# Eight result buffers instead of six, softmax weights made in place in PSUM, PSUM banks from a table, and another order of the matmul steps, in a gated mix of local attention and a Mish MLP

## The chip, the cores and the metric

The kernel runs on one core of a Trainium2 chip. The core has a matmul engine (TensorE, PE in the profile; its weight loads are PEld), a vector engine (VectorE, DVE), a scalar engine (ScalarE, ACT), GpSimd (POOL) and a queue engine (SyncE, SP) from which nearly all DMAs are issued. Each engine takes its instructions strictly in the order in which they were written for it, and waits on semaphores where one needs another's result. The matmuls accumulate in PSUM, which is used here as eight banks of 512 floats per partition; all else on the chip lies in SBUF. The metric is the device time of one execution in microseconds; 622.23 is the median of three runs of the kernel before (620.2 to 622.58).

## The reference: a gate between attention and an MLP

```python
S, D, H, Dh, W, dil, F = 2048, 640, 32, 20, 8, 2, 1728      # all fp32
g = sigmoid((x * gate_w).sum(-1, keepdims=True))
# a: each token attends to itself and the 7 tokens 2, 4, ... 14 before it
q, k, v = split_heads(x @ wqkv)
logits = einsum("bhsd,bhswd->bhsw", q, gathered(k)) * Dh ** -0.5      # masked where the index is negative
a = einsum("bhsw,bhswd->bhsd", softmax(logits), gathered(v)) @ wo
# b: dense, Mish, dense
h = x @ w1 + b1
b = (h * tanh(softplus(h))) @ w2
out = g * a + (1 - g) * b
```

Three groups of matrix products carry the work: the projections to q, k and v, the two of the MLP, and the one behind the attention. The attention itself is elementwise products and sums over a window of eight.

## The kernel before

**Matmuls.** An fp32 operand is kept as a pair of reduced-precision parts, a high half and a low half. ACT copies the operand to the high half (L444), and DVE or GpSimd subtracts that from it to get the low half (L447); this is `split`. A product of two pairs is three matmuls, high by high, high by low, low by high (`mm3`, L512 to L514): the stationary operand is the weights' for the MLP, so its low half is first read by the third. Where blocks allow it, the kernel forms a two-by-two block product with seven block products instead of eight. The sums of blocks that this needs are made ahead by DVE or GpSimd (`combined`, L1017), and between the products a partial sum is carried from one PSUM bank into the next: ACT copies a bank to another ("seed", L1144, and L879 in the steps c1), and DVE adds or subtracts a kept block (L826 in `sum_to`, L1162 in `added`).

**Stages.** The 2048 tokens are two halves P of two blocks of 512. The steps have names in a long string, ORDER, which is the order of PE. `u.U.i` is slot i of a unit U of the q, k and v projection (a unit is a quarter of the heads in one half); `p.2.j.a1` to `c3` make units 2 and 3 together by the seven products; `q.P.i.*` are the first MLP layer for a pair i of column groups; `x`, `rest`, `last` and others belong to the second layer and the output. In p.2.j the step a1 makes a block v and a3 a block u, which are stored to HBM (`store`); c0 fetches both again into one pair buffer by two DMAs (L871); c1 seeds a bank with u (ACT L879), accumulates onto it, and DVE makes a second bank as that bank minus v (L826); c2 and c3 go on in the first and second of the two banks. c2 writes the bank that L826 reads, so it can't start before L826 is done.

**Attention on DVE.** For two groups of 128 tokens and eight heads: product with the keys (L569), sum (L572); for four groups: maximum and difference (L590, L591); ACT makes the exponential (L592) and from it the weights times the gate, into a tile `pw` of SBUF (L596); DVE sums, inverts, and multiplies `pw` by the inverse into `pg` in PSUM (L603 to L605); then product with the values (L614, two), sum (L618) and a transpose (L525). ACT copies the queries of two groups to `qg` in PSUM ahead of L569 (L575).

**What sets the order.** PE's order is the string's. For DVE, ACT, GpSimd and SP a planner inside the kernel (`Plan.run`) plays the whole program through with an estimated duration for each task and emits, for each engine, the ready task of the lowest rank; a split or a sum with engine "ANY" goes to DVE or to GpSimd, by when PE will need it. Buffers come in rings, taken in turn and given back when their last reader is done: three banks `sb` and three `qb` of PSUM, 24 pair buffers (NPAIR), eight raw ones (NRAW), six result buffers `hb` (NH) and others. So any change of a ring, an estimate or the string moves instructions on all engines.

**Start.** `warm()` (L424 to L428) issues six matmuls of 512 columns on constants, four of 128 and three of 384, into the three sb banks, while the first DMAs are under way. Unit 0 follows with L708 and L674 (`first_slots`, `qkv_pass`).

## Time and profile before

| | us |
|---|---|
| median of three runs | 622.23 (620.2, 622.23, 622.58) |
| the profiled execution | 620.13 |
| its span | 618.4 |
| PE busy | 611.8 (99%) |
| DVE busy | 584.4 (95%) |
| ACT busy | 364.6 (59%) |
| GpSimd (POOL) busy | 312.0 (50%) |

A row of the timeline has the start and the duration in us, the engine, the line, the operation, the tiles (written, then read) and their shape; `x3` is a row of three instructions in a run, whose duration is from the first start to the last end. In brackets stands the idle time ahead of it and what ended it. Matmuls overlap in the pipeline: a row of one lasts 0.39, and the next starts 0.22 or 0.23 later. In a table by stretches, the numbers behind the two bounds are the busy time and count of PE, PEld, DVE, ACT and POOL, the granted clock, the share of the DMA engines and GB/s. In the waits, a row has the total, the number and the longest.

### The profile page before, as it was taken

Reading aid. Unit: us, or ns where it says so; the run is one execution under the profiler, and the core shown is the slowest. Engines: PE = TensorE matmul, PEld = TensorE weight load, DVE = VectorE, ACT = ScalarE, POOL = GpSimd, SP = SyncE. Lnnn points to the kernel's source line nnn. Section 1 sums busy time; section 2 is a strip of 40 time slices with the busy share of each in tenths; the row PEclk is TensorE's granted clock in tenths of the full one; section 3 lists DMA queues with packets and bytes.
Section 4 is the critical chain, followed back from the end, with each engine's and each line's share of the span. In section 5 each row is a group of like instructions: output and inputs, shape, how many; then the busy total and the mean of one; then the engine's idle time right before and its main releaser. Section 6 shows DMA issues by size and latency. Waiting matters only on the chain.

```text
span 618.4 us, 9150 instructions
## 1 busy us (share of the span) xinstructions
PE 611.8 (99%) x2719; PEld 508.5 (82%) x2719; DVE 584.4 (95%) x550; ACT 364.6 (59%) x854; POOL 312.0 (50%) x287
## 2 busy tenths in 40 slices
PE   9999999999989999999999999999999999999997
PEld 7888888888878888888888888888888888888886
DVE  8899999999999999999999999999999999989955
ACT  7677657666785466533483656867855633645420
POOL 1677748679675446653545327898227634001000
PEclk9999999999999999999999999999999999999999
DMA  9873775979997689996889748978978966889923
GB/s 321 235 217 116 227 253 158 264 237 322 309 288 219 195 253 274 280 265 161 212 249 345 222 122 275 283 197 256 287 245 247 242 175 187 261 270 291 275 86 119
DMA packets 100769, 145.95 MB, mean 236 GB/s; under 512 B 11552, under 2 KB 54560, under 8 KB 100496
## 3 DMA queue, kind: packets, MB, share of 16 engines
q1 hardware_dynamic: 97360, 139.61, 70.9%
q0 software_dynamic: 3072, 5.51, 6.3%
q8 instruction: 21, 0.34, 0.2%
q14 instruction: 28, 0.23, 0.1%
q10 hardware_dynamic: 288, 0.26, 0.1%
HBM read 91.33 MB, written 53.03 MB: 233 GB/s over the span
## 4 chain that ended last, share of the span: by engine, by line
PE 97%; DVE 1%; DMA 0%; issue 0%; SPq 0%; ACT 0%; DVEq 0%; ACTq 0%
PE qb L512 20%; PE qb L514 20%; PE qb L513 20%; PE sb L512 12%; PE sb L514 12%; PE sb L513 12%; PE qb L674 1%; PE sb L426 1%; DMA o<-ot 0%; DVE lg L572 0%; PE sb L519 0%; PE sb L518 0%; PE qb L519 0%; PE qb L518 0%; PE sb L674 0%
## 5 line engine op out<-in xcount | busy, mean ns | idle before, releaser
L447 POOL TENSOR_TENSOR pair<-raw,pair 128x512 fp32r<-128x512 f32 (+4 forms) x127 | 155.9, 1247 | 109.9 <-ACT pair L444 71.9
L513 PE MATMUL qb<-pair 128*128 128x512 f32 (+1 forms) x451 | 174.4, 387 | 0.0
L512 PE MATMUL qb<-pair 128*128 128x512 f32 (+1 forms) x451 | 174.4, 387 | 0.0
L514 PE MATMUL qb<-pair 128*128 128x512 f32 (+1 forms) x451 | 174.4, 387 | 0.0
L444 ACT ACTIVATE pair<-raw 128x512 fp32r<-128x512 f32 (+2 forms) x229 | 133.2, 607 | 59.9 <-DMA raw<-actt 13.8
L512 PE MATMUL sb<-pair 128*128 128x512 f32 (+2 forms) x326 | 126.2, 387 | 1.9 <-ACT sb L879 1.8
L513 PE MATMUL sb<-pair 128*128 128x512 f32 (+2 forms) x326 | 126.0, 387 | 0.0
L514 PE MATMUL sb<-pair 128*128 128x512 f32 (+2 forms) x326 | 126.0, 386 | 0.0
L513 PEld LDWEIGHTS qb<-pair 128*128 128x128 f32 x451 | 84.6, 188 | 16.6
L514 PEld LDWEIGHTS qb<-pair 128*128 128x128 f32 x451 | 84.6, 188 | 16.6
L512 PEld LDWEIGHTS qb<-pair 128*128 128x128 f32 x451 | 84.7, 188 | 16.5
L614 DVE TENSOR_TENSOR pr<-kvq,pg 128x1280 f32<-128x1280 f32 x64 | 93.5, 1484 | 0.9
L569 DVE TENSOR_TENSOR pr<-kvq,qg 128x2560 f32<-128x2560 f32 x32 | 89.9, 2809 | 1.7
L618 DVE TENSOR_REDUCE kvq<-pr 128x320 f32<-128x2560 f32 x32 | 90.2, 2819 | 0.9
L572 DVE TENSOR_REDUCE lg<-pr 128x128 f32<-128x2560 f32 x32 | 90.2, 2818 | 0.8
L447 DVE TENSOR_TENSOR pair<-raw,pair 128x512 fp32r<-128x512 f32 (+2 forms) x102 | 71.4, 721 | 4.2 <-ACT pair L444 4.0
L512 PEld LDWEIGHTS sb<-pair 128*128 128x128 f32 x326 | 61.2, 188 | 14.9 <-ACT sb L879 2.2
L513 PEld LDWEIGHTS sb<-pair 128*128 128x128 f32 x326 | 61.2, 188 | 12.3
L514 PEld LDWEIGHTS sb<-pair 128*128 128x128 f32 x326 | 61.2, 188 | 12.2
L680 ACT ACTIVATE kvq<-qb 128x320 f32<-128x320 f32 x55 | 24.0, 436 | 56.6 <-PE qb L514 56.6
L1017 POOL TENSOR_TENSOR hb<-hb 128x512 f32<-128x512 f32 x34 | 44.2, 1307 | 24.8 <-ACT hb L1150 11.1
L444 ACT ACTIVATE pair<-hb 128x512 fp32r<-128x512 f32 (+3 forms) x62 | 36.5, 589 | 5.1 <-PE sb L514 2.0
(161 smaller groups left out, 728.9 us busy)
## 6 DMA issues: line engine op xcount, KB each, us to landing
actt<-hb SPq DMA_DIRECT2D x52, 256.0 KB, 3.6
raw<-in_w SPq DMA_DIRECT2D x40, 256.0 KB, 3.8
act<-hb SPq DMA_DIRECT2D x38, 256.0 KB, 3.3
raw<-actt SPq DMA_DIRECT2D x37, 256.0 KB, 4.1
raw<-in_wq SPq DMA_DIRECT2D x36, 248.0 KB, 3.5
raw<-act SPq DMA_DIRECT2D x29, 256.0 KB, 2.7
raw<-in_x SPq DMA_DIRECT2D x23, 256.0 KB, 4.5
o<-ot SPq DMA_DIRECT2D x64, 80.0 KB, 3.4
```

The costliest lines, as they stand in the source:

```text
L426: nc.tensor.matmul(warm_banks[i % 3].t[:, :n], ones[:, :128], ones[:, :n], start=True, stop=True)
L444: a = add("ACT", act_ns(n), lambda: A.activation(hi(), raw(), AF.Copy), after, rank=rank, take=take, hold=hold)
L447: return (V if e == "DVE" else G).tensor_tensor(lo(), raw(), hi().bitcast(F32), op=OP.subtract)
L512: nc.tensor.matmul(ps, ah, bh, start=first, stop=False, skip_group_check=more)
L513: nc.tensor.matmul(ps, ah, bl, start=False, stop=False, skip_group_check=more)
L514: nc.tensor.matmul(ps, al, bh, start=False, stop=last, skip_group_check=more)
L569: return V.tensor_tensor(pr, window(kv, s0, 0), qg[:, :, None, :].to_broadcast([128, 2, W, QF]), op=OP.mult)
L572: V.tensor_reduce(lg_w[:, s0:s0 + 2], pr.rearrange("p s w (h d) -> p s w h d", d=DH), op=OP.add, axis=AX.X)
L614: V.tensor_tensor(pairs[:, s].rearrange("p k i (h d) -> p k i h d", d=DH), vw, pg[:, s0 + s].rearrange("p (k i) h -> p k i h", i=2)[:, :, ...
L618: V.tensor_reduce(q[:, s0:s0 + 2], pairs.rearrange("p s k i f -> p s f k i"), op=OP.add, axis=AX.XY)
L680: a = add("ACT", 330, lambda: A.activation(kv[:, 7 + s], ps.t[:, QF:3 * QF].rearrange("p (a b) -> p a b", a=2), AF.Copy), [done] + before, ...
L1017: return (V if e == "DVE" else G).tensor_tensor(t.t[:, i:i + n], a.t[:, j:j + n], b.t[:, k:k + n], op=op)
```

## The change

- The ring of result buffers goes from six to eight (NH). The room comes from dropping `pw`, from moving the maxima `mx` into the bank of `qg`, and from smaller constants (`bound`, `gc`, `gt`) and a smaller first kvq tile.
- ACT writes the weights straight into `pg` in PSUM, and DVE multiplies `pg` in place.
- A table BANKS says for 21 bank requests from which of the two rings they come (`bank_buf`); all others take the ring they had.
- ORDER is new in the first two thirds, around the steps c of p.2 and the turn from the first half of the tokens to the second above all, and differs in places after it.
- The three matmuls of 384 columns in `warm()` are gone; the four of 128 now accumulate.

All lines below L249 move by 1 to 3: L447 becomes L450, L569 L572, L572 L575, L826 L829, L871 L874, L879 L882, L1017 L1020, L1144 L1147, L1162 L1165.

```diff
-NPAIR, NRAW, NH = 24, 8, 6
+NPAIR, NRAW, NH = 24, 8, 8
+BANKS = {'q03al': 's', 'p23be': 'q', 'p21de': 's', 'q05ep': 's', 'q1111': 's', 'q1201': 'q', 'p23ga': 'q', 'u04': 's', 'q1400': 's', 'q1300': 's', 'u05': 's', 'l0': 's', 'u06': 's', 'q1000': 's', 'q1200': 's', 'u47': 's', 'u46': 's', 'q1100': 's', 'q1510': 'q', 'u40': 's', 'q1211': 's'}
...
-pieces.0.5 q.0.5.first q.0.4.l1 p.2.3.c0 q.0.5.m1 q.0.5.m4 q.0.5.second x.3.3 q.0.5.m2 x.2.1 x.3.0 p.2.0.c1 p.2.1.c1 x.3.4 p.2.0.c2 q.0.5.m3 p.2.3.c1
-p.2.2.c0 p.2.2.c1 q.0.5.l1 p.2.3.c2 x.2.2 p.2.3.c3 x.3.2 x.2.3 p.2.2.c3 p.2.2.c2 x.3.1 p.2.0.c3 p.2.1.c3 p.2.1.c2 x.2.4 q.0.5.l2 wq.4 x.2.0 third sum
...
+q.0.4.m1 p.2.2.c0 q.0.4.m3 q.0.4.m4 q.0.4.m2 q.0.4.l2 x.2.3 q.0.4.l1 q.0.5.first x.3.2 p.2.3.c1 x.3.3 wq.4 q.0.5.m1 q.0.5.second p.2.3.c2 q.0.5.m4
+p.2.1.c1 p.2.2.c1 p.2.0.c1 p.2.0.c3 p.2.2.c2 q.0.5.m2 p.2.0.c2 p.2.2.c3 x.2.4 x.2.0 sum p.2.3.c3 q.0.5.m3 p.2.1.c3 q.0.5.l1 p.2.1.c2 q.0.5.l2
...
+    def bank_buf(name, ring):
+        return sb_buf() if BANKS.get(name, ring) == "s" else qb_buf()
...
-    bound = keep.tile([1, HQ, 7], F32)
+    bound = keep.tile([1, 1, 1], F32)
-    gc = keep.tile([128, 2, 32], F32)
-    gt = keep.tile([128, 2, 32], F32)
+    gc = keep.tile([128, 32], F32)
+    gt = keep.tile([128, 32], F32)
...
-    kvq = [at.tile([128, 2 * KC * D], F32, name="kvq0"), pe.tile([128, 15 * ROW + 8 * QF], F32, name="kvq1"),
+    kvq = [at.tile([128, 6144], F32, name="kvq0"), pe.tile([128, 15 * ROW + 8 * QF], F32, name="kvq1"),
...
-    pw = at.tile([128, 8, W, HQ], F32, name="pw")
-    pw_h = pw.rearrange("p s w h -> p s h w")
-    qg = shared.tile([128, 2, QF], F32, name="qg")
+    pg_h = pg.rearrange("p s w h -> p s h w")
+    qm = shared.tile([128, 512], F32, name="qg")
+    qg = qm[:, :2 * QF].rearrange("p (s f) -> p s f", f=QF)
-    mx = at.tile([128, 8, HQ], F32, name="mx")
+    mx = qm[:, 2 * QF:2 * QF + 8 * HQ].rearrange("p (s h) -> p s h", h=HQ)
...
-            nc.tensor.matmul(warm_banks[i % 3].t[:, :n], ones[:, :128], ones[:, :n], start=True, stop=True)
-        for b in warm_banks:
-            nc.tensor.matmul(b.t[:, 128:], ones[:, :128], ones[:, 128:], start=False, stop=True, skip_group_check=True)
+            nc.tensor.matmul(warm_banks[i % 3].t[:, :n], ones[:, :128], ones[:, :n], start=i < WARM, stop=True, skip_group_check=True)
...
-                    A.activation(lg[0:1, s, :, 0:7 - s], bound[:, :, 0:7 - s], AF.Copy)
+                    A.activation(lg[0:1, s, :, 0:7 - s], bound.to_broadcast([1, HQ, 7 - s]), AF.Copy)
...
-                    A.activation(pw_h[:, i], lg[:, i], AF.Copy, scale=gate[:, P, i:i + 1])
+                    A.activation(pg_h[:, i], lg[:, i], AF.Copy, scale=gate[:, P, i:i + 1])
...
-            return t, step("DVE", 430, lambda: V.tensor_tensor(pg[:, h], pw[:, h], sm[:, h, None, :].to_broadcast([128, 4, W, HQ]), op=OP.mult), [copied])
+            return t, step("DVE", 430, lambda: V.tensor_tensor(pg[:, h], pg[:, h], sm[:, h, None, :].to_broadcast([128, 4, W, HQ]), op=OP.mult), [copied])
...
-            n, ep, v = self.n, qb_buf(), h_buf()
+            n, ep, v = self.n, bank_buf(f"p{self.u}{j}ep", "q"), h_buf()
...
-            n, al, be = self.n, qb_buf(), sb_buf()
+            n, al, be = self.n, bank_buf(f"p{self.u}{j}al", "q"), bank_buf(f"p{self.u}{j}be", "s")
...
-            ga, de, n = sb_buf(), qb_buf(), NCOL
+            ga, de, n = bank_buf(f"p{self.u}{j}ga", "s"), bank_buf(f"p{self.u}{j}de", "q"), NCOL
...
-            V.tensor_scalar(gc[:, P, :8], gate[:, P], -1.0, 1.0, op0=OP.mult, op1=OP.add)
-            V.transpose(gt[:, P], gc[:, P])
+            V.tensor_scalar(gc[:, :8], gate[:, P], -1.0, 1.0, op0=OP.mult, op1=OP.add)
+            V.transpose(gt, gc)
-                nc.sync.dma_start(g_d[P][:, 32 * i:32 * (i + 1)], gt[32 * i:32 * i + 8, P])
+                nc.sync.dma_start(g_d[P][:, 32 * i:32 * (i + 1)], gt[32 * i:32 * i + 8])
```

In what follows the numbers in tile names are the buffers' own, given anew in each program. DVE's order near 35 us, where it leaves the splits for the first product of the attention, before:

```order
L447 TENSOR_TENSOR pair_615<-raw_516,pair_615 128x512
L447 TENSOR_TENSOR pair_618<-raw_510,pair_618 128x512
L447 TENSOR_TENSOR pair_621<-raw_543,pair_621 128x512
L1017 TENSOR_TENSOR raw_647<-raw_581,raw_569 128x256
L1017 TENSOR_TENSOR raw_647<-raw_569,raw_647 128x256
L569 TENSOR_TENSOR pr_275<-kvq0_268,qg_274 128x2560
L572 TENSOR_REDUCE lg_271<-pr_275 128x2x8x8
```

and after:

```order
L450 TENSOR_TENSOR pair_601<-raw_511,pair_601 128x512
L450 TENSOR_TENSOR pair_625<-raw_505,pair_625 128x512
L450 TENSOR_TENSOR pair_628<-raw_538,pair_628 128x512
L1020 TENSOR_TENSOR raw_631<-raw_564,raw_631 128x256
L450 TENSOR_TENSOR pair_635<-raw_564,pair_635 128x512
L450 TENSOR_TENSOR pair_653<-raw_593,pair_653 128x512
L450 TENSOR_TENSOR pair_667<-raw_576,pair_667 128x512
L572 TENSOR_TENSOR pr_274<-kvq0_268,qg_273 128x2560
L575 TENSOR_REDUCE lg_271<-pr_274 128x2x8x8
L1165 TENSOR_TENSOR hb_732<-hb_705,sb_606 128x512
```

pair_615 and pair_601 are the same split, and so are pair_618 and pair_625, pair_621 and pair_628. A sum, raw_647, is now made from one part on GpSimd, and three more splits, pair_635 (the weights of q.0.1.first), pair_653 and pair_667, stand ahead of the first product; an add, L1165, stands behind the first pair of product and reduction.

PE's order at the same place, before, where the weights of q.0.1.first are pair_625 (its low half is made by GpSimd):

```order
L512 MATMUL qb_663<-kvq2_270,pair_449 128x512
L513 MATMUL qb_663<-kvq2_270,pair_449 128x512
L514 MATMUL qb_663<-kvq2_270,pair_449 128x512
L512 MATMUL qb_679<-kvq2_270,pair_625 128x512
L513 MATMUL qb_679<-kvq2_270,pair_625 128x512
L514 MATMUL qb_679<-kvq2_270,pair_625 128x512
```

and after, where they are pair_635:

```order
L515 MATMUL sb_606<-pair_601,pair_497 128x512
L516 MATMUL sb_606<-pair_601,pair_497 128x512
L517 MATMUL sb_606<-pair_601,pair_497 128x512
L515 MATMUL qb_660<-kvq2_270,pair_635 128x512
L516 MATMUL qb_660<-kvq2_270,pair_635 128x512
L517 MATMUL qb_660<-kvq2_270,pair_635 128x512
```

q.0.1.first follows another step, the second product of q.0.0, which reads pair_601. It comes nine matmuls sooner in the sequence: besides the warming ones, 133 matmuls stand ahead of it in after and 142 before.

DVE's order at the steps c1 of p.2, before:

```order
L447 TENSOR_TENSOR pair_2003<-raw_1949,pair_2003 128x512
L1162 TENSOR_TENSOR hb_2017<-hb_2009,sb_1890 128x512
L1162 TENSOR_TENSOR hb_2009<-hb_2009,sb_1932 128x512
L447 TENSOR_TENSOR pair_2020<-raw_1959,pair_2020 128x512
L590 TENSOR_REDUCE mx_276<-lg_271 128x32
L591 TENSOR_TENSOR lg_271<-lg_271,mx_276 128x256
L572 TENSOR_REDUCE lg_271<-pr_275 128x2x8x8
L826 TENSOR_TENSOR qb_2072<-sb_2029,pair_1741 128x496
L826 TENSOR_TENSOR qb_2075<-sb_2034,pair_1759 128x496
L826 TENSOR_TENSOR qb_2080<-sb_2046,pair_1861 128x496
```

and after:

```order
L575 TENSOR_REDUCE lg_271<-pr_274 128x2x8x8
L528 STREAM_TRANSPOSE ot_1976<-kvq1_269 128x4x5x32
L1165 TENSOR_TENSOR hb_1985<-hb_1965,sb_1881 128x512
L572 TENSOR_TENSOR pr_274<-kvq0_268,qg_273 128x2560
L1165 TENSOR_TENSOR hb_1965<-hb_1965,sb_1919 128x512
L829 TENSOR_TENSOR qb_2032<-qb_2003,pair_1936 128x496
L575 TENSOR_REDUCE lg_271<-pr_274 128x2x8x8
L829 TENSOR_TENSOR sb_2069<-sb_1999,pair_1616 128x496
```

Before, three differences (L826) stand in a row behind two adds, a maximum and a reduction. After, two adds stand on either side of an attention product, one difference (qb_2032) behind the second, and the next (sb_2069) behind a further reduction.

PE's order there, before, from the end of the third c1 to the first c3:

```order
L512 MATMUL sb_2046<-pair_1705,pair_618 128x496
L513 MATMUL sb_2046<-pair_1705,pair_618 128x496
L514 MATMUL sb_2046<-pair_1705,pair_618 128x496
L512 MATMUL sb_2029<-pair_1729,pair_434 128x496
L513 MATMUL sb_2029<-pair_1729,pair_434 128x496
L514 MATMUL sb_2029<-pair_1729,pair_434 128x496
L512 MATMUL qb_2072<-pair_1690,pair_577 128x496
L513 MATMUL qb_2072<-pair_1690,pair_577 128x496
L514 MATMUL qb_2072<-pair_1690,pair_577 128x496
```

and after, from the end of the second c1 to the first c3:

```order
L515 MATMUL sb_1999<-pair_1694,pair_625 128x496
L516 MATMUL sb_1999<-pair_1694,pair_625 128x496
L517 MATMUL sb_1999<-pair_1694,pair_625 128x496
L515 MATMUL qb_2003<-pair_1739,pair_429 128x496
L516 MATMUL qb_2003<-pair_1739,pair_429 128x496
L517 MATMUL qb_2003<-pair_1739,pair_429 128x496
L515 MATMUL qb_2032<-pair_1680,pair_572 128x496
L516 MATMUL qb_2032<-pair_1680,pair_572 128x496
L517 MATMUL qb_2032<-pair_1680,pair_572 128x496
```

Before, the three c1 (six matmuls each) follow on sb_2029, sb_2034 and sb_2046, all from the ring sb, and c2 on sb_2029 writes what L826 reads. After, the c1 of p.2.3 is on qb_2003 and comes ahead of that on sb_1999; c2 on qb_2003 follows these six matmuls, then c3 on qb_2032 and c3 on sb_2069, nine each. From the last matmul on sb_1881, which the first of the two adds reads, 24 matmuls are issued up to c2 on qb_2003, and 36 up to c3 on sb_2069.

SP's queue where u and v are fetched for c1 of p.2.3, before:

```order
L477 DMA actt2_0_3_142<-hb_1837 128x512
L871 DMA pair_1861<-pu2_3_261 128x496
L871 DMA pair_1861<-pv2_3_257 128x496
L477 DMA raw_1866<-in_x 128x512
L477 DMA actt4_0_3_170<-hb_1864 128x512
L477 DMA raw_1884<-in_x 128x512
```

and after:

```order
L480 DMA act22_0_4_115<-hb_1726 128x512
L480 DMA raw_1925<-in_wq 128x512
L874 DMA pair_1936<-pu2_3_261 128x496
L874 DMA pair_1936<-pv2_3_257 128x496
L480 DMA actt3_0_4_157<-hb_1864 128x512
L480 DMA actt2_0_4_143<-hb_1939 128x512
L480 DMA raw_1967<-in_wq 128x512
L874 DMA pair_1971<-pu2_2_260 128x496
L874 DMA pair_1971<-pv2_2_256 128x496
```

In both programs these two DMAs are the third of four such pairs. Before, the c1 of p.2.3 is also the third c1 on PE; after, it is the first, and the two DMAs stand behind raw_1925, five rows ahead of the pair for p.2.2.

More of the change, by code (lines that the diff above doesn't have):

```diff
@@ L267 @@
+u.7.3 rest.2 rest.3
 """
@@ L1838, in one @@
         def one(self, half, h):
-            ps = qb_buf() if half == h else sb_buf()
+            ps = bank_buf(f"q1{self.q}{half}{h}", "q" if half == h else "s")
             xs = [X[2 * self.P + h, kc] for kc in range(KC)]
```

43 lines of the change are left out of this document (21 added, 22 removed).

## The prediction

> **What bounds the kernel now.** I read the page's summary and chain first, then the busy time by stretches of 50 us, then the waits of TensorE (PE).
>
> ```profile
> span 618.4 us, 9150 instructions
> PE 611.8 (99%) x2719; PEld 508.5 (82%) x2719; DVE 584.4 (95%) x550; ACT 364.6 (59%) x854; POOL 312.0 (50%) x287
> PE 97%; DVE 1%; DMA 0%; issue 0%; SPq 0%; ACT 0%; DVEq 0%; ACTq 0%
> ```
>
> ```profile
> 0.00:50.00 50.00, 49.21 (x213) 39.53 (x214) 44.52 (x44) 33.98 (x84) 28.16 (x30) 1.00 0.77 245
> 50.00:100.00 50.00, 50.00 (x225) 41.87 (x224) 48.44 (x41) 34.42 (x79) 32.84 (x29) 1.00 0.64 199
> 150.00:200.00 50.00, 48.13 (x214) 39.58 (x213) 49.13 (x43) 36.26 (x97) 33.48 (x28) 1.00 0.87 284
> 550.00:600.00 50.00, 50.00 (x222) 41.39 (x221) 44.75 (x75) 24.61 (x44) 2.49 (x3) 1.00 0.76 239
> 600.00:618.40 18.40, 14.45 (x73) 12.14 (x71) 9.73 (x16) 1.20 (x2) 0.00 (x0) 0.94 0.26 100
> ```
>
> The first number behind the comma is PE's busy time. PE is full everywhere but in the first 50 us (0.8 lost at the start), between 150 and 200 (1.9 lost) and in the last stretch (4.0 after the last matmul). DVE, the third, is nearly full too, so PE and DVE bound the kernel together: a change gains only what PE now loses, 1.9 us at one place plus small change, and can lose wherever DVE hands PE something later. The waits say what the 1.9 us are:
>
> ```profile
> PE sb L512 <- ACT sb L879: 1.8, 1, 1.8
> ```
>
> The profiled execution took 620.13 us, its span 618.4. The three runs beside it gave 622.58, 620.2 and 622.23: two of four executions lie near 620.2 and two near 622.4. I make the sum against 620.13 and add 1.0 for the median of the changed kernel, half of the distance. Less than 0.5% (3.1 us) is about what a measurement of this kernel can't tell from no change; against the median of 622.23, faster begins at 619.1 and slower at 625.3.
>
> **Warming.** Three matmuls of 384 columns go.
>
> ```profile
> 0.79 3.15 PE L426 MATMUL sb<-const-bfloat16-1.0 128*128 128x512 bf16 x10 [0.79 <-PEq L1951]
> 3.73 1.17 PE L428 MATMUL sb<-const-bfloat16-1.0 128*128 128x384 bf16 x3
> 3.93 0.29 DVE L1739 CAST pair<-raw 128x256 fp32r<-128x256 f32 x1 [0.43 <-DMA raw<-in_wq]
> 4.15 0.36 DVE L1747 CAST kvq<-raw 128x384 fp32r<-128x384 f32 x1
> 4.45 0.88 PE L708 MATMUL qb<-pair,kvq 128*128 128x256 f32 x2
> 5.13 0.75 PE L674 MATMUL qb<-pair,kvq 128*128 128x512 f32 x2
> 7.95 0.68 PE qb L674 x3
> ```
>
> The last row is of the chain, whose pieces don't overlap: three matmuls of 512 columns in 0.68, 0.227 each. L426's six of 512 and four of 128, 3584 columns, took 0.79 to 3.73, which is 0.42 for 512: the array starts at half rate, and the spacing turns to 0.23 at about 5.3 us. The three L428 are 1152 columns, 0.95 us at that rate: the most that can be saved. But the second L708 needs L1739 (end 4.22), and the first L674 needs L1747 (end 4.51). So L708 can start at 3.8, L674 at about 4.55 instead of 5.13; nearly two L674 then run at half rate, where before less than one did, 0.2 us more. I take -0.4 (0 to -0.95). [...]
>
> **The weights of q.0.1, earlier.** The order of DVE at the start shows the largest new cost. In before the low half of the weights (pair_625) is made by GpSimd; now (pair_635) by DVE, behind pair_601, pair_625, pair_628 and raw_631.
>
> ```profile
> 32.44 3.54 DVE L447 TENSOR_TENSOR pair<-raw,pair 128x512 fp32r<-128x512 f32 x3
> 35.90 0.87 DVE L1017 TENSOR_TENSOR raw<-raw 128x256 f32<-128x256 f32 x2
> 36.86 2.82 DVE L569 TENSOR_TENSOR pr<-kvq,qg 128x2560 f32<-128x2560 f32 x1
> 33.78 1.65 POOL L447 TENSOR_TENSOR pair<-raw,pair 128x512 fp32r<-128x512 f32 x1 [0.66 <-ACT pair L444]
> 34.98 0.39 PE L512 MATMUL qb<-pair 128*128 128x512 f32 x1
> 37.48 0.39 PE L514 MATMUL qb<-kvq,pair 128*128 128x512 f32 x1
> 37.59 5.03 POOL L447 TENSOR_TENSOR pair<-raw,pair 128x512 fp32r<-128x512 f32 x4 [2.16 <-ACT pair L444]
> ```
>
> In before GpSimd was done at 35.43, and the third product (L514), the first to read that half, came at 37.48: no wait. In after the same product stands nine matmuls of 0.227, or 2.0 us, sooner; its triple starts where the row of 34.98 stands, so it is due at 34.98 + 0.45 - 0.4 = 35.0. DVE's row at 32.44 holds three splits, the counterparts of pair_601, pair_625 and pair_628; the third ended where the next row starts, 35.9, and by the lengths of 1.2, 0.7 and 1.8 into which the row falls the first ended at 33.67. Behind it come two more of 0.69, a quarter-size sum of 0.43 and the split wanted: 0.69 + 0.69 + 0.43 + 0.69 = 2.5, so 36.2 undisturbed. DVE's rows of this stretch are not undisturbed (3.54 for three, where one alone is 0.69); with one op lengthened by 1.1 it is 37.3. I take 36.6, between them: PE waits +1.5 (0.9 to 2.4), and all that is behind it on PE with it. [...]
>
> ```profile
> 26.65 0.69 DVE L447 TENSOR_TENSOR pair<-raw,pair 128x512 fp32r<-128x512 f32 x1
> 27.26 1.80 DVE L1017 TENSOR_TENSOR raw<-raw 128x512 f32<-128x512 f32 x1
> 27.22 1.30 POOL L447 TENSOR_TENSOR pair<-raw,pair 128x512 fp32r<-128x512 f32 x1 [1.12 <-ACT pair L444]
> ```
>
> [...]
>
> **Attention begins later.** Two further splits (pair_653, pair_667) stand ahead of the first L572, formerly L569 at 36.86: 36.6 + 2 x 0.69 = 38.0, and 0.7 for one of the two lengthened in part, 38.7. Against a PE that itself lost 1.5 - 0.4 = 1.1 this is 0.7 late, and L1165 hb_732 comes right behind one product and one reduction (2.82 each): +0.3 (0 to 1).
>
> **The turn of units 2 and 3.**
>
> ```profile
> 170.85 1.47 DVE L1162 TENSOR_TENSOR hb<-hb,sb 128x512 f32<-128x512 f32 x2
> 172.06 1.59 ACT L879 ACTIVATE sb<-pair 128x496 f32<-128x496 f32 x3
> 172.69 0.49 PE L512 MATMUL sb<-pair 128*128 128x496 f32 x1 [1.77 <-ACT sb L879]
> 173.62 2.81 DVE L572 TENSOR_REDUCE lg<-pr 128x128 f32<-128x2560 f32 x1
> 176.35 1.83 DVE L826 TENSOR_TENSOR qb<-sb,pair 128x496 f32<-128x496 f32 x3
> 177.07 0.50 PE L512 MATMUL sb<-pair 128*128 128x496 f32 x1
> ```
>
> Three seeds (ACT L879) wait for banks that DVE's two adds (L1162) free, and PE has nothing else: 1.93 lost, the 1.77 of the row and the later spacing of its restart. After 18 more matmuls PE would be at 176.8, but the next writes a bank that the first L826 still reads, behind the reduction (176.35 + 0.61 = 176.96): it started at 177.07, 0.26 late. Together 2.19. In after one seed goes to a free bank of the other ring, so the first wait goes. What is late next is L829: the chain on DVE from the last matmul on sb_1881 is L1165 0.68, L572 2.81, L1165 0.68, L829 0.61 = 4.8, against 24 matmuls, 12 of 0.227 and 12 of 0.222, 5.4: it holds by 0.3 after latency. The next L829 (sb_2069) comes after one more reduction: 4.8 + 2.8 + 0.6 = 8.2, and 0.2 of latency, against 36 matmuls, 8.0: PE waits 0.4. Two later sums, each behind a long DVE op, I give 0.3 apiece. So 2.19 - 1.0 = -1.2 (-2.2 to 0).
>
> **Softmax weights in PSUM.**
>
> ```profile
> 280.89 1.13 ACT L596 ACTIVATE pw<-lg,gate 128x64 f32<-128x64 f32 x4
> 290.58 0.43 DVE L605 TENSOR_TENSOR pg<-pw,sm 128x256 f32<-128x256 f32 x1
> L605 DVE TENSOR_TENSOR pg<-pw,sm 128x256 f32<-128x256 f32 x16 | 7.8, 486 | 0.9
> L1162 DVE TENSOR_TENSOR hb<-hb,sb 128x512 f32<-128x512 f32 x12 | 8.2, 683 | 1.4 <-PE sb L514 0.6 <-ACT pair L444 0.5
> L447 DVE TENSOR_TENSOR pair<-hb,pair 128x512 fp32r<-128x512 f32 x30 | 20.4, 684 | 0.0
> ```
>
> A DVE op with a PSUM operand (683 ns) costs what one without has (684), so L605 stays at 0.43. ACT now writes the tile that DVE multiplies in, 8.6 us ahead of L605; it must wait for the last reader of that half, one group back, long done. I take 0; the bounds are the 16 L605 by the 0.06 between the single row and their mean, either way, -0.9 to +0.9. The maxima in PSUM: the same rows, 0.
>
> **Eight buffers, banks, the small constants.** No wait of PE on a result buffer stands in the waits, so two more give nothing by themselves; the banks' effect is in the turn. From 200 us to the last stretch PE is full before, so the new order can gain nothing there, and I see no hand-over that it makes late: 0.
>
> Sum: -0.4 + 1.5 + 0.3 - 1.2 + 0 + 0 = +0.2: 620.3 for an execution like the profiled one, 621.3 with the 1.0 for the median.
>
> **Rivals.** *Faster:* DVE reaches pair_635 in time, as the planner means it, and the seeds and sums of the turn leave no wait: -0.4 - 2.2 = -2.6, 617.5 like the profiled run, 617.5 to 619.6 as median. For it: the turn's chain misses by 0.4 alone. Against: 2.5 us of DVE work have to fit into 1.3.
> *Slower, DVE held by GpSimd:* GpSimd is busy beside all four ops of that chain, each of the three large ones takes 1.80 instead of 0.69 and the small one 0.6 more: 3 x 1.1 + 0.6 = 3.9 later than 36.2, PE waits 5.1 in place of 1.5, 623.9 and up to 626.0 as median. It decides from 4.4 us of waiting where the runs fall on the upper of the two levels, from 5.5 in between. For it: 3.54 for three; against: GpSimd idled 2.16 us behind its op of 33.78.
> *Slower, the reload comes late:* the u and v of p.2.3 are fetched just ahead of their seed.
>
> ```profile
> 162.79 0.32 SPq L871 DMA_DIRECT2D pair<-pu  x1
> DMA to landing us min/median/max: 2.5/3.9/4.9
> ```
>
> The second row is over all of L871's: up to 4.9 us to land, a seed's copy 0.6 more, and in before PE used this one 10 us after its issue. In after the pair follows raw_1925 in SP's queue, which waits for a buffer that a split frees; I put the issue at 160.5 and the seed's use at 168.6. If it slips by 5 us to 165.7, 4.9 + 0.6 make PE wait up to 2.6: 622.9, as median up to 625.0, and more with a later issue.
> [...]
> *The eight buffers do nothing:* this is in the forecast.
>
> **Chances.** Forecast 0.48, faster rival 0.18, GpSimd's hold 0.18 (0.15 of it beyond 0.5%), the reload 0.12 (0.07 of it), the clock 0.04. Faster 0.18; slower 0.15 + 0.07 = 0.22; same 0.60. The range leaves out 0.1 at each end: 618.0 keeps half and more of the faster rival, 625.5 all but the far end of the two slow ones.
>
> **What would show it.** The first L711 near 3.8 and full rate by 5.4; a wait of PE on DVE L450 of 0.9 to 2.4 near 35; L572 first at 38 to 39; near 170 no wait on ACT L882 and one or two under 0.5 on L829; PE busy 50.00 in every later stretch. The forecast is wrong if PE is full at 35, if a stretch behind 200 us has lost PE time, or if DVE's busy time moves by more than 2 us.

## The result: 0.17% faster, and another chain

Over 22 executions of each, the changed kernel takes 619.45 us (median; 619.14 to 621.44) and the kernel before 620.47 (619.45 to 622.58): a ratio of 0.9983, 95% interval 0.9976 to 0.9990. That is 1.0 us, within the 0.5% of the forecast's "same" and 1.9 under the 621.3 forecast. The profiled execution took 619.46, its span 617.7, 0.7 less than before.

The page of the changed kernel, its busy times and its chain:

```profile
span 617.7 us, 9122 instructions
PE 611.9 (99%) x2716; PEld 508.1 (82%) x2716; DVE 580.3 (94%) x546; ACT 370.0 (60%) x856; POOL 316.7 (51%) x291
PE 87%; DVE 7%; ACT 2%; DMA 2%; issue 2%; SPq 0%; DVEq 0%; ACTq 0%
```

PE's busy time is what it was. DVE's fell by 4.1 us and GpSimd's rose by 4.7: of the sums `hb` (L1017, now L1020) DVE makes 9 instead of 14, 3.5 us less. The chain changed too: 97% PE and 1% DVE before, 87% and 7% now. The same stretches as before (start and end, PE's busy time first behind the comma):

```profile
0.00:50.00 50.00, 48.35 (x205) 38.20 (x206) 45.01 (x46) 35.58 (x83) 25.80 (x28) 1.00 0.72 237
50.00:100.00 50.00, 49.88 (x224) 41.62 (x223) 47.09 (x40) 33.24 (x80) 32.37 (x28) 1.00 0.67 207
150.00:200.00 50.00, 49.88 (x222) 41.24 (x221) 49.23 (x45) 37.50 (x100) 34.90 (x30) 1.00 0.93 297
```

The 1.9 lost between 150 and 200 is 0.1; 0.9 more is lost in the first 50 us, and 0.1 between 50 and 100. PE's timeline has the places:

```profile
35.01 0.39 PE L516 MATMUL qb<-kvq,pair 128*128 128x512 f32 x1
36.20 0.49 PE L517 MATMUL qb<-kvq,pair 128*128 128x512 f32 x1 [0.80 <-DVE pair L450]
44.69 0.49 PE L515 MATMUL sb<-kvq,pair 128*128 128x512 f32 x1
61.49 0.39 PE L517 MATMUL qb<-kvq,pair 128*128 128x512 f32 x1
62.01 0.50 PE L515 MATMUL sb<-pair 128*128 128x512 f32 x1
177.06 0.38 PE L517 MATMUL qb<-pair,kvq 128*128 128x496 f32 x1
177.56 0.49 PE L515 MATMUL sb<-pair 128*128 128x496 f32 x1
```

Undisturbed, the next start comes 0.22 or 0.23 later; what is more is lost, with some 0.1 for the restart behind it. Taken so, over all starts:

| place (us) | what PE waits for | before | after |
|---|---|---|---|
| 35 to 36 | DVE's split of q.0.1's weights | 0 | 1.07 |
| 45 | DVE's add on hb_732 | 0 | 0.10 |
| 61.5 | a seed (ACT L1147) behind DVE's add on hb_705 | 0 | 0.39 |
| 67 | | 0.10 | 0 |
| 170 | seeds of c1 (ACT) | 2.04 | 0 |
| 177 | a difference (DVE L826, L829) | 0.37 | 0.38 |
| sum | | 2.51 | 1.94 |

With 0.20 gained at the start this is 0.77; the last matmul starts 0.65 earlier (613.52 against 614.17), and I don't place the 0.1 between.

The table has to add up, since PE issues the same matmuls in both. It reads like a balance in which the wait at 36 costs 1.07 of the 2.04 gained, so that without this wait the kernel would be 1.07 faster. The chain between 29 and 62 us contradicts that:

```profile
34.52 0.68 DVE pair L450
35.20 0.35 DVE raw L1020
35.69 0.47 issue
36.17 0.62 ACT pair L447
36.78 0.32 ACT kvq L683
37.73 0.49 ACT sb L1147
38.37 2.82 DVE pr L572
...
60.74 0.61 DVE hb L1165
61.37 0.59 ACT sb L1147
62.01 0.50 PE sb L515
```

PE is not in it. The end is set by DVE's run of splits and attention up to the add of 60.74, with some copies of ACT between 36.2 and 38.2; the wait at 36 lies beside that run. Which of the two readings holds, the experiments had to tell.

### The profile page after: what moved, and what is told of

Its sections match the earlier page's. It is cut to its first block, busy times and chain, and to the rows that moved or that the text cites. A ratio compares the mean times of both kernels' runs of the same rounds, so it can differ in the third digit from the quotient of the medians.

```text
span 617.7 us, 9122 instructions
## 1 busy us (share of the span) xinstructions
PE 611.9 (99%) x2716; PEld 508.1 (82%) x2716; DVE 580.3 (94%) x546; ACT 370.0 (60%) x856; POOL 316.7 (51%) x291
## 4 chain that ended last, share of the span: by engine, by line
PE 87%; DVE 7%; ACT 2%; DMA 2%; issue 2%; SPq 0%; DVEq 0%; ACTq 0%
PE qb L516 16%; PE qb L517 16%; PE qb L515 16%; PE sb L515 12%; PE sb L516 12%; PE sb L517 12%; DVE pr L572 2%; DVE lg L575 2%; DMA act<-hb 1%; DVE pair L450 1%; DVE raw L1020 1%; PE qb L677 1%; ACT hb L1153 1%; DVE hb L1165 1%; DMA ot<-o 1%
## 5 line engine op out<-in xcount | busy, mean ns | idle before, releaser
L450 POOL TENSOR_TENSOR pair<-raw,pair 128x512 fp32r<-128x512 f32 (+4 forms) x128 | 157.1, 1247 | 111.9 <-ACT pair L447 60.3
L447 ACT ACTIVATE pair<-raw 128x512 fp32r<-128x512 f32 (+2 forms) x229 | 132.8, 606 | 66.7 <-DMA raw<-actt 20.4
L517 PE MATMUL qb<-pair 128*128 128x512 f32 (+1 forms) x403 | 155.7, 386 | 0.0
L516 PE MATMUL qb<-pair 128*128 128x512 f32 (+1 forms) x403 | 155.7, 386 | 0.0
L515 PE MATMUL qb<-pair 128*128 128x512 f32 (+1 forms) x403 | 155.7, 386 | 0.0
L515 PE MATMUL sb<-pair 128*128 128x512 f32 (+2 forms) x374 | 144.9, 388 | 0.2
L517 PE MATMUL sb<-pair 128*128 128x512 f32 (+2 forms) x374 | 144.7, 387 | 0.0
L516 PE MATMUL sb<-pair 128*128 128x512 f32 (+2 forms) x374 | 144.7, 387 | 0.0
L572 DVE TENSOR_TENSOR pr<-kvq,qg 128x2560 f32<-128x2560 f32 x32 | 89.9, 2811 | 2.4 <-ACT qg L578 1.3
L575 DVE TENSOR_REDUCE lg<-pr 128x128 f32<-128x2560 f32 x32 | 90.2, 2818 | 0.7
L515 PEld LDWEIGHTS qb<-pair 128*128 128x128 f32 x403 | 75.6, 188 | 14.8
L516 PEld LDWEIGHTS qb<-pair 128*128 128x128 f32 x403 | 75.7, 188 | 14.7
L517 PEld LDWEIGHTS qb<-pair 128*128 128x128 f32 x403 | 75.6, 188 | 14.6
L515 PEld LDWEIGHTS sb<-pair 128*128 128x128 f32 x374 | 70.2, 188 | 15.3 <-ACT sb L1147 0.5
L516 PEld LDWEIGHTS sb<-pair 128*128 128x128 f32 x374 | 70.2, 188 | 14.1
L517 PEld LDWEIGHTS sb<-pair 128*128 128x128 f32 x374 | 70.2, 188 | 14.1
L450 DVE TENSOR_TENSOR pair<-raw,pair 128x512 fp32r<-128x512 f32 (+2 forms) x101 | 70.1, 715 | 2.6 <-ACT pair L447 2.3
L1020 POOL TENSOR_TENSOR hb<-hb 128x512 f32<-128x512 f32 x39 | 50.5, 1304 | 22.0 <-ACT hb L1153 12.7
L683 ACT ACTIVATE kvq<-qb 128x320 f32<-128x320 f32 x50 | 21.8, 436 | 50.1 <-PE qb L517 49.8
L447 ACT ACTIVATE pair<-hb 128x512 fp32r<-128x512 f32 (+3 forms) x62 | 36.5, 589 | 1.5 <-PE qb L517 1.2
```

What stands on the lines that cost most here:

```text
L447: a = add("ACT", act_ns(n), lambda: A.activation(hi(), raw(), AF.Copy), after, rank=rank, take=take, hold=hold)
L450: return (V if e == "DVE" else G).tensor_tensor(lo(), raw(), hi().bitcast(F32), op=OP.subtract)
L515: nc.tensor.matmul(ps, ah, bh, start=first, stop=False, skip_group_check=more)
L516: nc.tensor.matmul(ps, ah, bl, start=False, stop=False, skip_group_check=more)
L517: nc.tensor.matmul(ps, al, bh, start=False, stop=last, skip_group_check=more)
L572: return V.tensor_tensor(pr, window(kv, s0, 0), qg[:, :, None, :].to_broadcast([128, 2, W, QF]), op=OP.mult)
```

## Experiments

"Ledger theory" is the table read as a balance, in which a wait taken away is gained; "chain theory" says that up to 62 us only what shortens DVE's chain counts. Lines of the experiments' kernels are shifted by a few where code was added.

### The three warming matmuls, put back and taken out alone

```diff
# put back into the changed kernel
-            nc.tensor.matmul(warm_banks[i % 3].t[:, :n], ..., start=i < WARM, ...)
+            nc.tensor.matmul(warm_banks[i % 3].t[:, :n], ..., start=True, stop=True)
+        for b in warm_banks:
+            nc.tensor.matmul(b.t[:, 128:], ones[:, :128], ones[:, 128:], start=False, ...)
# taken out of the kernel before: the reverse
```

> The changed kernel with the three warming matmuls of 384 columns put back, all else as changed. Ledger theory (the changed kernel gains 0.2 at the start, because the first real matmuls then run at half rate themselves): the first matmul on the second block of weights comes at about 7.8 instead of 7.6, the span goes from 617.7 to 617.9, no difference that the time can show. Rival A (all of their 0.95 us was saved): 618.6. Rival B (without them the clock comes up later): the span falls below 617.5.

> The kernel before with only the three warming matmuls taken out. Ledger theory: the matmul at 7.78 comes at about 7.58, the span goes from 618.4 to 618.2, and the losses of PE near 170 and 177 (2.04 and 0.37) stay. Rival A (0.95 saved): 617.5.

Put back: span 618.0, median 619.84 (ratio to before 0.9991, 0.9982 to 1.0000), the first matmul on the second block of weights at 7.83. Taken out: span 618.1, 620.38 (1.0004, 0.9991 to 1.0017), that matmul at 7.69:

```profile
7.69 0.85 PE L672 MATMUL qb<-pair,kvq 128*128 128x512 f32 x3
```

So 0.1 to 0.3 and not 0.95, as the ledger theory had it; rivals A and B did not come. Over all profiles of this study that start is at 7.44, 7.78 and 7.83 with the three matmuls, and without them between 7.42 and 8.11 in nine, 8.64 and 10.00 in two: what is gained in one is no larger than the scatter, and the two late ones cost more. In both of them PE paused: in the one of 10.00 for 0.71, for DVE's L1742, ahead of 4.97, most of which, by my estimate, the three matmuls would have covered (with them the same matmul starts at 4.91 in the kernel before), in the one of 8.64 for 1.24 just ahead of that moment, which they would not have.

### Parts of the change alone

Three kernels take apart order, buffers and PSUM.

```diff
# old early steps: the changed kernel, with steps 1 to 32 of ORDER as before
# old order and banks: the changed kernel, with
-BANKS = {'q03al': 's', ...}
+BANKS = {}
 ORDER = (that of before)
# PSUM only: as old order and banks, and
-NPAIR, NRAW, NH = 24, 8, 8
+NPAIR, NRAW, NH = 24, 8, 6
```

> The changed kernel with the first 32 steps of ORDER as before (q.0.1.first late again), all later steps, the banks, the buffers and the warming as changed. Ledger theory (the wait on DVE's split near 36 costs 1.07 and has nothing to do with the turn): PE has no wait near 35, the loss near 177 stays at or under 0.4, the span falls from 617.7 to 616.5 +- 0.3, the time by 0.2% under the changed kernel. Rival (the early steps were moved because the turn needs it): a loss of 1 to 2 us comes back at the steps c1, and the span is 617.5 or more.

> All of the change but the order and the banks: eight result buffers, weights in place in PSUM, maxima in PSUM, fewer warming matmuls, with ORDER as before and every bank from its old ring. Ledger theory (buffers and PSUM give nothing by themselves, the turn's gain is the order's): PE loses about 2 us near 170 again, span 618.2 +- 0.3. Rival (the two buffers or the PSUM tile give the gain): the loss near 170 is under 1 us, span 617.5 or less. Third possibility (the weights in place cost): DVE's busy time rises by more than 1 us and PE loses time behind 200 us.

> The kernel before with the weights made in place in PSUM, the maxima in PSUM, the small constants and the shorter warming, but six result buffers, its own ORDER and its own banks: every engine has the order of before. With the run of the shorter warming alone it shows what the PSUM part costs, and with the run of all but order and banks what the two buffers do under the old order. Theory P (the PSUM part is free): span 618.1 +- 0.2, as with the shorter warming alone, DVE's busy time within 1 us of it, PE's losses near 170 and 177 as there. Rival (the PSUM part is what cost the run with old order and banks its 4 us): span above 620.

*Old early steps:* 627.62, ratio 1.0116 (1.0100 to 1.0132), span 625.4. The wait at 36 is gone, as the ledger theory expected, and the kernel is 8 us slower: losses of 0.8 and 1.0 near 122 and 129 and of 0.7, 2.0 and 2.4 between 170 and 182. The rival had the sign, with a larger size. From the first changed step on, the planner gives DVE, ACT and GpSimd another order (DVE has 558 instructions instead of 546), and I take it that the later steps are no longer served as the string was made for; which task came late I did not follow up.

*Old order and banks:* 626.73, ratio 1.0109 (1.0089 to 1.0128), span 622.7, where the theories had 618.2 and 617.5 or less. The third possibility came in part: DVE's busy time is 587.1, and 0.3 is lost at 331. *PSUM only:* 621.29, ratio 1.0016 (1.0002 to 1.0029), span 619.0. Both have the order of before in the string; PSUM only has it on every engine, and the other differs from it by the two buffers alone. Those cost 3.7 us of span in the profiled executions, and 5.4 by the medians, since the profiled execution of old order and banks is the fastest of its six. The planner spends them: result buffers that come free earlier let other tasks be emitted first, and at the turn two of the three seeds now stand on ACT behind the softmax's exponential and weights (old order and banks, ACT, then PE, then DVE):

```profile
172.95 0.59 ACT L882 ACTIVATE sb<-pair 128x496 f32<-128x496 f32 x1
173.56 1.28 ACT L595 ACT_TABLE_LOAD   x1
175.30 1.37 ACT L599 ACTIVATE pg<-lg,gate 128x64 f32<-128x64 f32 x4
176.61 1.07 ACT L882 ACTIVATE sb<-pair 128x496 f32<-128x496 f32 x2
173.59 0.49 PE L515 MATMUL sb<-pair 128*128 128x496 f32 x1 [2.35 <-ACT sb L882]
177.04 0.78 PE L515 MATMUL sb<-pair 128*128 128x496 f32 x1 [1.84 <-DVE qb L829]
176.31 0.67 DVE L829 TENSOR_TENSOR qb<-sb,pair 128x496 f32<-128x496 f32 x1
```

PE, with one seeded bank instead of three, has 6 matmuls ahead of its c2 where it had 18, and then waits for L829, which stands behind a reduction of 2.81. So the string fixes PE's order only as far as the planner finds its steps ready in time: a step that is ready overtakes one that isn't. In the kernel before, too, the c1 of p.2.3 stands ahead of c2 of p.2.0, which the string has first.

The buffers are no gain by themselves; they are what the new string needs. With seven or six the planner comes to a point where no task of that string can go on, so there is no time for the string with fewer buffers.

PSUM only against the shorter warming alone (span 618.1) is 0.9 slower, 0.17 of it at the start and 0.35 at 83 us; the rest comes in pieces of under 0.1 between 88 and 572, which I did not follow up. What comes ahead of the loss at 83 stands on DVE:

```profile
70.20 1.49 DVE L617 TENSOR_TENSOR pr<-kvq,pg 128x1280 f32<-128x1280 f32 x1
73.19 1.49 DVE L617 TENSOR_TENSOR pr<-kvq,pg 128x1280 f32<-128x1280 f32 x1 [1.50 <-ACT pg L599]
```

The second product reads weights that were ready for the first, and waits 1.50 for ACT, which writes those of the next groups into the other half of pg: the program waits for the whole tile, not for the half. With pw in SBUF these two products stand in one row of 2.89 without a pause. Theory P is wrong, its rival too: the PSUM part costs 0.4 to 0.8 under this order, not 4.

### The new turn alone, and one bank less

```diff
# turn only: the kernel before, with steps 66 to 139 of ORDER as in the changed kernel
# one bank less: the changed kernel, with
-BANKS = {..., 'p23ga': 'q', ...}
+BANKS = {..., ...}
```

> The kernel before, six result buffers, weights in SBUF, old banks and old warming, with only the steps 65 to 138 of ORDER (from the first c0 of p.2 to the first steps of the second half) as in the changed kernel. Theory B (the order of the steps needs the bank table): PE loses 1.5 us or more at the steps c1, waiting for a seed by ACT L879, span 618.5 or more. Rival (order alone): the losses between 165 and 185 are under 0.6, span 616.5 to 617.2.

> The changed kernel with one entry fewer in the table of banks: the seeded bank of p.2.3.c1 comes from the ring sb again. Up to the turn all engines have the order of the changed kernel. Theory B (the gain at the turn is that this seed finds a free bank in the other ring): PE loses 1.5 us or more near 170, waiting for a seed by ACT L882, span 619 or more. Rival (the order of the steps alone makes the gain): the loss from 168 to 180 stays under 0.6, span 617.5 to 618.0.

Turn only: 631.88, ratio 1.0182 (1.0165 to 1.0199). One bank less: 641.42, ratio 1.0332 (1.0318 to 1.0347). Neither the steps without the table nor the table without this entry gives the gain. PE waits for a seed, as theory B had it, but not for the reason that theory B gave, a bank that isn't free. One bank less, ACT and PE; then turn only, ACT and PE:

```profile
170.98 0.59 ACT L882 ACTIVATE sb<-pair 128x496 f32<-128x496 f32 x1 [0.22 <-DMA pair<-pu]
171.62 0.78 PE L515 MATMUL sb<-pair 128*128 128x496 f32 x1 [5.64 <-ACT sb L882]
```

```profile
167.86 0.59 ACT L879 ACTIVATE sb<-pair 128x496 f32<-128x496 f32 x1 [0.83 <-DMA pair<-pu]
168.50 0.78 PE L512 MATMUL sb<-pair 128*128 128x496 f32 x1 [4.08 <-ACT sb L879]
```

In both the first seed of the turn waits for the fetch of u, issued at 165.33 and at 164.96, when PE was there or nearly so. In the changed kernel it is issued little earlier, and takes longer than any in before (the second row is over all four pairs):

```profile
164.03 0.66 SPq L874 DMA_DIRECT2D pair<-pu  x1
DMA to landing us min/median/max: 2.7/3.7/5.9
170.78 0.57 ACT L882 ACTIVATE qb<-pair 128x496 f32<-128x496 f32 x1
```

It landed at 169.9, and PE used the seeded bank at 172.0, 0.65 after the seed's end. What differs is PE's own order. Without the warming ones, 739 matmuls stand ahead of the first on a seeded bank in the changed kernel, and 706 in each of the other two; in one bank less PE's order is the changed kernel's up to there. So PE is there 33 matmuls, or some 7.5 us, sooner, and the fetch isn't. Whether it is the free bank that lets these 33 go first, and how much of the gain is theirs, stays open: the entry moves PE's order and all that follows together.

### The wait at 36, taken away without another plan

Here the order of one engine is changed behind the planner's back, and that of all others stays word for word.

```diff
# split ahead: the splits 23 and 24 on DVE (pair_625, pair_628) are emitted behind the 25th (pair_635)
+            if splits[0] in (23, 24):
+                held_back.append(emit)
+                return None
...
+            if splits[0] == 25:
+                while held_back:
+                    i = held_back.pop(0)(V)
# and to GpSimd: besides, the 27th (pair_667) is emitted on GpSimd
```

> The changed kernel with one move on DVE: the split of pair_635, for which PE waits near 36, ahead of the splits of pair_625 and pair_628, which PE needs at 43 and 54. All else stands as in the changed kernel. Ledger theory (the wait near 36 costs 1.07): the wait goes and the span falls from 617.7 to 616.6. Chain theory (from 29 to 61 us the chain that sets the end runs over DVE and ACT, so the wait near 36 lies beside it): the wait goes, but PE then loses as much more where it waits for DVE's adds, near 44.7 and at 61.5, and the span stays at 617.7 +- 0.15.

> As the run with the split of pair_635 moved ahead, and besides the split of pair_667, the last one ahead of the first attention product, goes from DVE to GpSimd at the same place. Chain theory: the first attention product starts at about 37.7 instead of 38.4, the adds near 44 and 61 come 0.7 earlier, and the span falls by 0.4 to 0.7, to 617.0 to 617.3, against 617.7 with the first move alone. Ledger theory: no more than the first move alone gave, 616.6. Third possibility: DVE lags again by the turn, and the loss near 177 grows by what was gained: 617.7.

Split ahead: 619.42, the changed kernel's 619.45 again (ratio to before 0.9988, 0.9979 to 0.9997). PE has no wait at 36, and waits at 45 instead:

```profile
43.92 0.39 PE L530 MATMUL qb<-pair 128*128 128x512 f32 x1
45.21 0.50 PE L528 MATMUL sb<-kvq,pair 128*128 128x512 f32 x1 [0.90 <-DVE hb L1178]
```

That is 1.18 lost where 0.10 was, and 0.40 at 62 as before. The ledger theory is out, the chain theory holds: to take the 1.07 away gained nothing. (The span is 618.2; this execution was 0.52 behind the changed kernel's already at the second matmul of q.0.1.first, which starts at 35.53 against 35.01.)

And to GpSimd: 619.83, no gain where 0.4 to 0.7 was expected. With the first move alone the five splits took 4.19 and the product started at 38.90, in an execution that ran 0.5 late from the start; here four take 4.68:

```profile
34.10 4.68 DVE L452 TENSOR_TENSOR pair<-raw,pair 128x512 fp32r<-128x512 f32 x4
38.71 2.81 DVE L585 TENSOR_TENSOR pr<-kvq,qg 128x2560 f32<-128x2560 f32 x1
34.98 4.93 POOL L452 TENSOR_TENSOR pair<-raw,pair 128x512 fp32r<-128x512 f32 x3 [1.08 <-ACT pair L449]
```

Two of DVE's four take 0.68 and two 1.78, and these two run beside GpSimd's: the second of them, at 37.01, beside the moved split itself, 1.74 at 36.50. So what DVE was spared came back on its next split; that GpSimd's ops lengthen DVE's is read from such lengths alone. Moving this split did not shorten the chain.

### What does shorten the chain

DVE has one pause of its own in the chain, new with the change (changed kernel, DVE, then ACT):

```profile
53.80 0.43 DVE L593 TENSOR_REDUCE qg<-lg 128x32 f32<-128x256 f32 x1
54.73 0.42 DVE L594 TENSOR_TENSOR lg<-lg,qg 128x256 f32<-128x256 f32 x1 [0.51 <-ACT qg L578]
54.26 0.44 ACT L578 ACTIVATE qg<-kvq 128x320 f32<-128x320 f32 x1 [2.51 <-DVE qg L593]
```

L594 needs the maxima that L593 wrote, and waits for ACT's copy of the next queries, which goes to other columns of the same tile (hence the name qg in L593's row); that the shared tile is the reason is what the first of the next runs tests. Another pause of 0.51 stands at 113.9.

```diff
# maxima in SBUF: the changed kernel, with
-    mx = qm[:, 2 * QF:2 * QF + 8 * HQ].rearrange("p (s h) -> p s h", h=HQ)
+    mx = at.tile([128, 8, HQ], F32, name="mx")
-    keep.tile([128, 118], F32, name="gap")
+    keep.tile([128, 54], F32, name="gap")
# adds earlier: besides, the split ahead as above, and on DVE
#   L572, L575, L1165 hb_732        ->  L572, L1165 hb_732, L575
#   L575, L572, L1165 hb_705, L575  ->  L575, L1165 hb_705, L572, L575
# difference earlier: besides, on DVE
#   L829 qb_2032, L575, L829 sb_2069  ->  L829 qb_2032, L829 sb_2069, L575
```

> The changed kernel with the maxima mx back in a tile of their own in SBUF (64 floats taken from the unused gap tile); every engine keeps the order of the changed kernel. Tile theory (the maxima share a tile with qg, so the difference L594 waits for ACT's next write of qg, which writes other columns): the pauses of 0.51 on DVE ahead of L594 near 54.7 and 113.9 go, the add near 61 comes 0.5 earlier, PE's loss of 0.39 at 61.5 goes, and the span falls to 617.3 +- 0.2. Rival (the pauses are hidden, as predicted): 617.7 and the loss at 61.5 stays.

> The changed kernel with the split of pair_635 ahead of two others, the maxima in SBUF, and two adds (L1165 on hb_732 and on hb_705, for which PE waits near 44 and 61) each one place earlier on DVE, ahead of a reduction and of a product of the attention. Chain theory (PE and DVE wait for each other in turn, and what counts is where the adds stand): PE's losses at 36, 44.7 and 61.5 all go, 1.5 us; the one near 177 stays, 0.4; span 616.2 to 616.8, a time 0.2% under the changed kernel. Rival (DVE is the bound up to the turn, so any order of the same work ends alike): the losses come back between 62 and 180, span 617.4 or more.

> The kernel of the run before (split ahead, maxima in SBUF, two adds earlier), and besides the difference L829 on sb_2069, for which PE waits near 177, one place earlier on DVE, ahead of the reduction of 2.82 us. Chain theory (the place on DVE is what PE waits for): the loss of 0.39 near 177 goes and none over 0.2 takes its place, span 616.5 +- 0.2 where the clock comes up as early as in that run. Rival (DVE is late by then in any order): the loss moves to the next differences near 181 to 186, span 616.9.

Maxima in SBUF: 619.01, ratio 0.9981 (0.9969 to 0.9993). L593 and L594 follow each other without a pause, and the loss at 61.5 is gone:

```profile
56.03 0.41 DVE L593 TENSOR_REDUCE mx<-lg 128x32 f32<-128x256 f32 x1
56.47 0.42 DVE L594 TENSOR_TENSOR lg<-lg,mx 128x256 f32<-128x256 f32 x1
```

From the 100th to the 300th matmul PE gains 0.43 on the changed kernel, about as large as the loss that went. The tile theory holds; in the time, the gain can't be told from none (0.9981 against 0.9983, intervals that overlap). (The profiled execution itself took 621.49; in it the matmuls came 0.43 apart until 9.67, which the last section shows.)

Adds earlier: 618.68, ratio 0.9965 (0.9952 to 0.9978), span 616.9, the fastest of all: 0.35% under the kernel before, where the changed kernel is 0.17% under it (their intervals just touch). The losses at 36, 45 and 61.5, 1.56 together, are gone; two of 0.2 have come at 49 and 107, which I didn't follow up. Ahead of the second add DVE now waits for PE, and not PE for DVE (DVE's row, then the page's chain):

```profile
59.09 0.69 DVE L1186 TENSOR_TENSOR hb<-hb,sb 128x512 f32<-128x512 f32 x1 [1.54 <-PE sb L530]
PE 97%; ACT 1%; DVE 1%; DMA 1%; issue 0%; SPq 0%; DVEq 0%
```

The chain is PE's again, 97%. The span is 0.1 above what the chain theory gave; its rival is out. Three moves are made at once here, so what each of them gives stays open.

Difference earlier: 619.13, ratio 0.9978 (0.9968 to 0.9988), span 617.4. The loss at 177 goes, and 0.87 comes at 181.6 and 184.5:

```profile
185.22 0.49 PE L528 MATMUL qb<-pair 128*128 128x496 f32 x1 [0.37 <-DVE qb L851]
174.06 0.68 DVE L851 TENSOR_TENSOR sb<-sb,pair 128x496 f32<-128x496 f32 x1 [0.64 <-PE sb L530]
```

The rival had the place and too small a size. Its reason, that DVE is late in any order, is not what the second row shows: one place earlier the difference isn't ready, DVE stands idle 0.64 for PE's matmul, and the differences behind come that much later. An order in which it doesn't idle wasn't tried.

## Why the prediction was right, and where it was not

The time lay in the range, the change within 0.5%, on the better side of nothing instead of 0.2 worse. The range of 618.0 to 625.5 was seven times as wide as the change of 1.0, so that the time lay in it says little for the single steps, whose errors went both ways and in part cancelled. One of the three signs that the prediction named for being wrong came: DVE's busy time moved by 4.1 us, where over 2 was named, and the forecast had no term for tasks that the planner gives to GpSimd instead. Its steps by measurement:

- **What bounds the kernel.** "PE and DVE bound the kernel together" was the useful sentence. As an account the sum of PE's waits is in order: the measured ones give -0.20 + 1.07 + 0.49 - 2.03 - 0.10 = -0.77, against +0.2, so that forecast and result differ by the sizes, the turn's (0.8) and that of q.0.1 (0.4) above all. What the sum can't tell is what a wait is worth if it is taken away: the split ahead showed that a wait of PE beside a DVE chain is worth nothing alone, and the adds earlier that several go at once when DVE's order is changed at the right places.
- **Warming**, -0.4: measured -0.1 to -0.3 in the runs made for it, in the range; the late starts of two profiles without the three matmuls, at 8.64 and 10.00, had no term in the sum.
- **The weights of q.0.1, earlier**, +1.5 (0.9 to 2.4): the wait came where and why it was said, 1.07 long, because fewer of DVE's ops were lengthened (2.97 for three, not 3.54). To take it away alone gained nothing. The rival in which GpSimd holds DVE did not come: the split for which PE waited took 0.68, from 35.46, and GpSimd's next op began at 36.34. That a DVE op beside GpSimd's takes longer was read from two rows of before, 1.80 beside its 1.30 against 0.69 ahead of it.
- **Attention begins later**, +0.3 (0 to 1): the product started at 38.37 (38.7 foretold). The add on hb_732 cost 0.10; the next one, on hb_705, 0.39, and that was on the chain. The step stopped one add too early.
- **The turn of units 2 and 3**, -1.2 (-2.2 to 0): measured 2.41 less 0.38, -2.03. The one wait worked out from the rows, 0.4 for sb_2069, is 0.38; the two put in without rows, 0.3 apiece, didn't come. One reading was off: the seeds of before did not wait for DVE's adds alone. The first add ended at 171.54, and ACT was at a split and a step of the Mish, without a pause, until its first seed at 172.06.
- **Softmax weights in PSUM**, 0: this step failed, by its reason and its size. It looked for the last reader of a half and took the half as what is waited for; the program waits by tile. Maxima that share a tile with qg cost 0.51 on DVE twice and 0.4 of PE's time in the profile; pg halves that share one cost 1.5 on DVE and 0.35 on PE under the old order. Its bounds went by a mean of 486 ns that one L605 of 1.32 us had made; the other fifteen took 0.42 to 0.44, as all sixteen do after.
- **Eight buffers**, 0: by themselves they cost 3.7 of span under the old order (5.4 by the medians), and the new order can't do without them. "Give nothing by themselves" was read from PE's waits; what a ring does to the planner's order isn't in those.
- **The reload rival** was closer than its 0.12: the fetch was issued at 164.0, not 160.5, and landed 0.86 before the seed's copy began, which ended 0.65 before PE used the bank. In two neighbours of this kernel, in which PE comes to the seed 33 matmuls sooner, it is a wait of 4 to 6 us.
- **The 1.0 added for the median** was wrong. Four executions looked like two levels, half on each; over 22 the kernel before lies at 620.47, near its profiled 620.13. Without it the forecast is 620.3, 0.9 from the result.

The faster rival asked that DVE reach pair_635 in time and that the turn leave no wait; neither came true, and its 617.5 wasn't reached.

## What to carry to other kernels

Where two engines are both full, a wait of one is no gain to be had unless the chain that ended last runs through it (the 1.07 at 36, taken away, left 619.42 for 619.45): look the stretch up in the chain before counting on it, and to gain there move the one instruction that the other engine waits for ahead of a long one, but not ahead of its own input. Two things in one PSUM tile waited for each other here even in different columns (0.51 on DVE twice, 1.50 once), so a buffer that is moved into another's tile needs its neighbours' writers read too. And in a kernel whose order a planner makes, a part of a change taken alone is another kernel: hold the order fixed, engine by engine, and move one instruction, to learn what that one is worth.

## What the hardware showed that was not expected

The moment at which the matmul starts go from 0.43 apart to 0.23 was not the same in all executions. In the profile of the kernel with the maxima in SBUF they stayed 0.43 apart until 9.7 us:

```profile
4.97 0.58 PE L711 MATMUL qb<-pair,kvq 128*128 128x256 f32 x1 [0.71 <-DVE pair L1742]
8.39 1.48 PE L677 MATMUL qb<-pair,kvq 128*128 128x512 f32 x3
9.67 0.49 PE L677 MATMUL sb<-pair,kvq 128*128 128x512 f32 x1
```

Starts 0.43 apart up to 9.67, against full rate, 0.23 apart, from 5.3 in the changed kernel: 4.4 us later, 2.4 us lost in all. The clock column has 1.00 for this stretch (5.4 to 9.7) all the same, so the rate is read from the starts. Ahead of it stands the pause of 0.71, ended by DVE's cast L1742. That it is the cause isn't shown: pauses of 0.64 and 0.56 at the same place, in the kernel before without its three matmuls and in the one with the adds earlier, had full rate by 5.4. Three of this kernel's twelve executions lie 2.2 to 2.5 above the median, and two of the changed kernel's 22 lie 1.8 to 2.0 above; whether all of them are late starts no trace shows. The 0.04 that the prediction gives the clock stands for a start like this one. Of the profiles of this study thirteen have full rate from between 4.8 and 6.5 us on, and this one from 9.7.

The rate also fell back in some runs. Behind two stalls of 2.7 and 2.2 us within 6.2 us, in the kernel with old order and banks, the matmuls came 0.41 apart from 177.62 to 179.69, and the clock column has 0.50 about there:

```profile
177.10:179.70 2.60, 2.60 (x7) 2.10 (x8) 2.60 (x1) 1.59 (x6) 0.96 (x2) 0.50 1.05 373
```

One stall of 2.16 in the kernel before had no such trail, and neither had stalls of 1.5 and 2.4 within 5.2 us in the kernel with one bank less. Single ones of 4.5, in the new turn alone, and of 6.0 and 6.5, in one bank less, had one, and so had one of 2.6 that began 5.3 us after another of 2.2 had ended, in old early steps. With a trail, the stall cost 1.4 to 1.9 us more than its length; what brings one on the runs don't settle.
